# Moving a query projection beside V in a two-branch attention kernel: row layout, VectorE denominators, crossbar transposes, one output accumulation, and a new start

## The chip, the cores and the metric

The kernel runs on one core of one Trainium2 chip. The metric is device time in microseconds (us), the median over executions.

Names: PE is TensorE's matmuls, PEld its weight loads, DVE is VectorE, ACT is ScalarE, POOL is GpSimd, SP is SyncE, which here only issues DMAs. SPq is SP's instruction queue. PSUM is the memory that TensorE writes, in banks, which the kernel uses as tiles of up to 128 x 512 fp32 values; to evict a bank is to copy its result out with VectorE or ScalarE, after which it can be filled again. The granted clock is the share of full speed that TensorE was allowed, as the profile records it (PEclk). In the views, `pk`, `pq` and `kqt` are keys and queries, `KVT` the kv blocks, `oB` the banks of the windowed attention's results, `Ob` the evicted results and `OBT` their transposes, which a DMA makes; a name with `_ps` is a PSUM bank. `L153` is line 153 of that run's kernel.

## The reference

One input x (2048 x 1024) goes through two attention blocks, and a gate per row mixes the results.

```python
g = sigmoid((x * gate_w).sum(-1, keepdims=True))
a = A(x, A_wqkv, A_wo)      # linear attention, 32 heads of 32
b = B(x, B_wqkv, B_wo)      # 8 keys per query, dilation 2, softmax
return g * a + (1 - g) * b

# A: phi(t) = where(t > 0, t + 1, exp(t)) + 1e-6
#    kv = phi(k)^T v ;  z = sum over rows of phi(k)
#    o = phi(q) kv / (phi(q) . z + 1e-6) ; then @ wo
```

## The kernel before

TensorE's program is in manual order. It goes through these stages: A's keys (`pk`, from x transposed and half of `WkA` at a time), G = x^T pk, the blocks kv and the sums z, B's values V, B's keys and queries (`kq`) with the windowed attention woven in, A's queries, then the two output projections. All other engines' instructions are ordered by the framework's scheduler.

The start: the first tiles of x come through the DMA crossbar, which transposes them on the way; all of `WkA` is loaded at the same time from another queue.

```python
WkA = load_w("WkA", A_wqkv, D, eng=nc.scalar, parts=2)
for s0, s1_ in ((0, 128), (128, 256), (256, 512), (512, 1024), (1024, 1536), (1536, S)):
    nc.sync.dma_start_transpose(out=xT[:, :, s0:s1_], in_=rows(x, s0, s1_))
for t in range(0, NB, 4):
    nc.sync.dma_start(out=xrow[:, t:t + 4, :], in_=...)        # x again, as rows
```

The key stage. `phi` is one ScalarE and two VectorE instructions per PSUM bank. The z sums (`zacc`) and the gate's dot products (`gjunk`) come later in the program, but nothing keeps them there on VectorE:

```python
for half in range(2):
    for t in range(NB):
        pj = ps_1.tile([P, 512], F32, name="pk_ps", tag="p1")
        for kt in range(KT):
            nc.tensor.matmul(pj[:], lhsT=xT[...], rhs=WkA[half][:, kt, :], ...)
        phi(pk[:, t, half * 512:(half + 1) * 512], pj)
# ... G matmuls ...
for t in range(2, NB):
    nc.vector.tensor_tensor(out=zacc[:], in0=zacc[:], in1=pk[:, t, :], op=ALU.add)
for tb in range(NB):
    nc.vector.tensor_tensor_reduce(out=gjunk[:], in0=xrow[:, tb, :], in1=gw_row[:], ...)
```

The kv blocks, four in one PSUM bank:

```python
kvp = ps_1.tile([P, 4, P], F32, name="kv_ps", tag="p1")
for i in range(4):
    for kt in range(KT):
        nc.tensor.matmul(kvp[:, i, :], ...)
    nc.vector.tensor_tensor(out=KVT[:, half * 4 + i, :], in0=kvp[:, i, :], in1=bdmask[:], op=ALU.mult)
```

A's denominators take a matmul each, with the queries transposed (columns are rows of x); the two projections get a bank each:

```python
nc.tensor.matmul(den[:], lhsT=Zb[:, c, :], rhs=pq[b][:, c, :], start=True, stop=True)
nc.scalar.activation(out=ld[:], in_=den[:], func=ACT.Ln, bias=eps[:])
nc.scalar.activation(out=ld[:], in_=ld[:], func=ACT.Exp, scale=-1.0)
nc.vector.tensor_tensor(out=pqs[:, b, c, :], in0=pq[b][:, c, :], in1=ld[:], op=ALU.mult)
# ... output tile: side 0 = B, side 1 = A, one bank each
nc.scalar.activation(out=st["ob"][:], in_=st[0][:], func=ACT.Copy, scale=omgall[:, tb:tb + 1])
nc.vector.scalar_tensor_tensor(out=osb[:], in0=st[1][:], scalar=gall[:, tb:tb + 1], in1=st["ob"][:], ...)
```

The softmax here doesn't subtract the row's maximum and nothing guards it: scores larger than these inputs give would overflow.

## Time and profile before

| | before |
|---|---|
| median time | 518.13 us (518.01 to 519.95, 3 runs) |
| profiled span | 517.1 us |
| PE busy | 494.4 us, 96% |
| first stage (keys) ends | 72.75 us; its 256 matmuls at full rate would take 55.3 us |

The stretches of the kernel before, one line per stage. The columns are the stretch, its length, the busy time of each engine with its number of instructions, the granted TensorE clock, the DMA share and the rate. In order: keys, G, kv and z, V, k/q with attention, the last attention block with a quarter of A's queries, the rest of A's queries with the output, the tail.

```profile
core 0: us, PE busy (x) PEld busy (x) DVE busy (x) ACT busy (x) POOL busy (x), PEclk, DMA share, GB/s
0.00:72.75 72.75, 59.76 (x257) 25.78 (x258) 46.65 (x90) 19.20 (x31) 4.53 (x23) 0.98 0.89 249
72.75:128.00 55.25, 55.25 (x260) 25.11 (x258) 21.07 (x33) 9.97 (x18) 0.00 (x0) 1.00 0.06 20
128.00:136.50 8.50, 6.21 (x82) 5.48 (x79) 2.33 (x8) 0.58 (x1) 0.00 (x0) 1.00 0.42 135
136.50:195.30 58.80, 58.80 (x274) 26.64 (x273) 11.59 (x24) 18.37 (x32) 3.57 (x4) 1.00 0.32 94
195.30:333.30 138.00, 136.93 (x1509) 66.44 (x1508) 90.26 (x236) 73.71 (x103) 0.00 (x0) 1.00 0.25 59
333.30:354.40 21.10, 18.60 (x222) 8.94 (x220) 18.14 (x49) 12.33 (x18) 0.00 (x0) 1.00 0.16 30
354.40:513.30 158.90, 158.84 (x736) 71.81 (x734) 71.85 (x116) 75.24 (x120) 0.00 (x0) 1.00 0.08 27
513.30:517.10 3.80, 0.00 (x0) 0.00 (x0) 0.75 (x1) 0.00 (x0) 0.00 (x0) 1.00 0.10 35
```

The G stage gives the rate at full clock: 256 matmuls of 512 columns in 55.25 us, 0.216 us each. TensorE's waits, who waited for whom, with total (us), number of times and longest:

```profile
PE pk_ps L153 <- DMA xT<-in_A_x_dram: 12.0, 2, 9.6
PE kv_ps L191 <- DVE KVT L194: 2.3, 6, 0.4
PE oB L315 <- DVE Ob L324: 2.2, 2, 1.2
PE q_ps L362 <- DVE pq_3522 L140: 1.3, 2, 0.9
PE pk_ps L153 <- DVE pk L140: 0.8, 3, 0.4
```

The start on TensorE's timeline (start, length, what, then the idle time before it and what ended it). In between, the matmuls ran 427 ns apart, at half rate, until about 19.5 us.

```profile
9.55 3.41 PE L153 MATMUL pk_ps<-WkA_72,xT 128*128 128x512 bf16 x8 [9.55 <-DMA xT<-in_A_x_dram]
15.44 14.81 PE L153 MATMUL pk_ps<-WkA_72,xT 128*128 128x512 bf16 x60 [2.47 <-DMA xT<-in_A_x_dram]
```

This is a piece of the chain of waits, the work that ended last followed back (start, length, what):

```profile
27.77 5.42 DMA xrow<-in_A_x_dram
33.33 1.22 DVE gjunk L179
34.90 1.13 DVE gjunk L179
36.04 0.60 DVE pk L140
```

The chain does not run through TensorE here. It runs through the load of x as rows, then through VectorE, where a gate product (`gjunk`) stands ahead of key evictions (`pk`). TensorE itself hardly waited for VectorE (0.8 us in all), because it was late for other reasons.

### The profile page before, as it was taken

How to read it: one execution, taken by the hardware profiler on the slowest of the kernel's cores; microseconds unless marked ns; L12 is line 12 of the kernel's file. 1: busy time of each engine (PE TensorE's matmuls, PEld its weight loads, DVE VectorE, ACT ScalarE, POOL GpSimd, SP SyncE). 2: the span in 40 equal slices, each digit the busy share in tenths (PEclk: the TensorE clock that was granted, in tenths of full speed). 3: DMA queues.
4: the chain of work that ended last, by engine and by line, in shares of the span. 5: the costliest groups of instructions: out<-in, count | busy, mean ns of one | idle time of the engine just before them, and what ended most of it. 6: DMA issues, size and time to landing. Idle time of an engine off the chain costs nothing.

```text
span 517.1 us, 8148 instructions
## 1 busy us (share of the span) xinstructions
PE 494.4 (96%) x3328; PEld 230.2 (45%) x3328; DVE 262.6 (51%) x553; ACT 209.4 (40%) x323; POOL 8.1 (2%) x27
## 2 busy tenths in 40 slices
PE   2899999999899999999999999989999999999996
PEld 0344444444544444444544544444444444444443
DVE  0459999200331101577766777698742653454221
ACT  0223331111133332555564555566872364256111
POOL 3000000000200000000000000000000000000000
PEclk9899999999999999999999999999999999999999
DMA  8999820000432226011171111111010000001101
GB/s 196 239 345 354 269 82 1 0 0 1 163 91 75 92 78 206 10 34 29 33 189 33 31 28 34 35 28 23 1 41 32 10 31 32 22 10 42 41 32 41
DMA packets 61333, 39.21 MB, mean 76 GB/s; under 512 B 36400, under 2 KB 56880, under 8 KB 61296
## 3 DMA queue, kind: packets, MB, share of 16 engines
q1 hardware_dynamic: 59104, 36.34, 25.4%
q10 hardware_dynamic: 2112, 2.10, 1.5%
q8 instruction: 26, 0.43, 0.4%
q0 software_dynamic: 80, 0.26, 0.2%
q14 instruction: 11, 0.09, 0.1%
HBM read 21.23 MB, written 4.19 MB: 49 GB/s over the span
## 4 chain that ended last, share of the span: by engine, by line
PE 82%; DVE 9%; SPq 5%; DMA 3%; issue 1%; ACT 0%; DVEq 0%
PE d_ps L410 21%; PE kq_ps L266 21%; PE v_ps L237 11%; PE g_ps L165 11%; PE d_ps L362 8%; SPq L96 5%; PE oB L315 3%; DVE pk L140 2%; DVE gjunk L179 2%; DMA OBT<-Ob 2%; DVE e L139 1%; PE q_ps L362 1%; PE den L395 1%; DMA xrow<-in_A_x_dram 1%; PE pk_ps L153 1%; PE kv_ps L191 1%
## 5 line engine op out<-in xcount | busy, mean ns | idle before, releaser
L165 PE MATMUL g_ps<-pk,xrow 128*128 128x512 bf16 x256 | 55.4, 379 | 0.0
L420 DVE SCALAR_TENSOR_TENSOR osb<-d_ps,gall,ob 128x512 bf16<-128x512 f32 x32 | 24.0, 748 | 49.0 <-PE d_ps L410 42.6
L153 PEld LDWEIGHTS <-xT 128*128 128x128 bf16 x256 | 25.6, 101 | 46.7 <-DMA xT<-in_A_x_dram 12.7
L153 PE MATMUL pk_ps<-WkA_72,xT 128*128 128x512 bf16 x128 | 31.7, 409 | 12.8 <-DMA xT<-in_A_x_dram 12.0
L272 DVE CAST kqt<-kq_ps 128x512 bf16<-128x512 f32 x32 | 21.7, 679 | 42.5 <-PE kq_ps L266 42.2
L139 DVE TENSOR_SCALAR e<-e 128x512 f32<-128x512 f32 x64 | 26.6, 421 | 32.1 <-ACT e L138 32.1
L416 ACT ACTIVATE ob<-d_ps,omgall 128x512 f32<-128x512 f32 x32 | 21.9, 683 | 48.4 <-PE d_ps L410 48.4
L138 ACT ACTIVATE e<-pk_ps 128x512 f32<-128x512 f32 x32 | 19.1, 597 | 54.9 <-DVE pk L140 27.4
L410 PEld LDWEIGHTS <-OBT 128*128 128x128 bf16 x256 | 25.1, 98 | 30.2
L165 PEld LDWEIGHTS <-xrow 128*128 128x128 bf16 x256 | 25.0, 98 | 30.2
L410 PEld LDWEIGHTS <-pqs 128*128 128x128 bf16 x256 | 25.0, 98 | 30.2
L237 PEld LDWEIGHTS <-xT 128*128 128x128 bf16 x256 | 25.1, 98 | 30.0
L324 DVE TENSOR_TENSOR Ob<-oB,rd 128x256 bf16<-128x256 f32 x80 | 31.4, 393 | 3.8 <-DMA OBT<-Ob 2.6
L266 PE MATMUL kq_ps<-xT,WkB_103 128*128 128x512 bf16 x128 | 32.9, 380 | 0.0
L266 PE MATMUL kq_ps<-xT,WqB_570 128*128 128x512 bf16 x128 | 32.9, 379 | 0.0
L266 PE MATMUL kq_ps<-xT,WkB_101 128*128 128x512 bf16 x128 | 32.3, 379 | 0.0
L266 PE MATMUL kq_ps<-xT,WqB_568 128*128 128x512 bf16 x128 | 32.2, 379 | 0.0
L410 PE MATMUL d_ps<-WoA_93,pqs 128*128 128x512 bf16 x128 | 31.7, 379 | 0.0
L410 PE MATMUL d_ps<-WoB_3861,OBT 128*128 128x512 bf16 x128 | 31.2, 379 | 0.0
L410 PE MATMUL d_ps<-WoB_3859,OBT 128*128 128x512 bf16 x128 | 30.7, 379 | 0.0
L410 PE MATMUL d_ps<-WoA_95,pqs 128*128 128x512 bf16 x128 | 30.7, 379 | 0.0
L237 PE MATMUL v_ps<-WvB_99,xT 128*128 128x512 bf16 x128 | 30.6, 379 | 0.0
(161 smaller groups left out, 650.9 us busy)
## 6 DMA issues: line engine op xcount, KB each, us to landing
xrow<-in_A_x_dram SPq DMA_DIRECT2D x4, 1024.0 KB, 9.8
out_dram<-osb SPq DMA_DIRECT2D x32, 128.0 KB, 1.9
WkA_72<-in_A_wqkv_dram ACTq DMA_DIRECT2D x2, 512.0 KB, 6.2
WkA_75<-in_A_wqkv_dram ACTq DMA_DIRECT2D x2, 512.0 KB, 12.2
WvA_89<-in_A_wqkv_dram SPq DMA_DIRECT2D x1, 1024.0 KB, 15.4
WvA_91<-in_A_wqkv_dram SPq DMA_DIRECT2D x1, 1024.0 KB, 17.8
WoA_93<-in_A_wo_dram SPq DMA_DIRECT2D x1, 1024.0 KB, 12.4
WoA_95<-in_A_wo_dram SPq DMA_DIRECT2D x1, 1024.0 KB, 11.8
```

Source lines behind the costliest of these rows:

```text
L96: nc.sync.dma_start_transpose(out=xT[:, :, s0:s1_], in_=rows(x, s0, s1_))
L139: nc.vector.tensor_scalar(out=e[:], in0=e[:], scalar1=1.0, scalar2=1e-6, op0=ALU.min, op1=ALU.add)
L153: nc.tensor.matmul(pj[:], lhsT=xT[:, kt, t * P:(t + 1) * P], rhs=WkA[half][:, kt, :], start=(kt == 0), stop=(kt == KT - 1))
L165: nc.tensor.matmul(pj[:], lhsT=xrow[:, t, kt * P:(kt + 1) * P], rhs=pk[:, t, half * 512:(half + 1) * 512], start=(t == 0), stop=(t == NB - 1))
L237: nc.tensor.matmul(st["pj"][:], lhsT=xT[:, kt, t * P:(t + 1) * P], rhs=WvB[half][:, kt, :], start=(kt == 0), stop=(kt == KT - 1))
L266: nc.tensor.matmul(st["pj"][:], lhsT=W[c // 4][:, kt, (c % 4) * P:(c % 4 + 1) * P], rhs=xT[:, kt, cols], start=(kt == 0), stop=(kt == KT - 1))
L272: nc.vector.tensor_copy(out=kqt[:, 1, cols], in_=st["pj"][:])
L324: nc.vector.tensor_tensor(out=Ob[:, 2 * b:2 * b + m], in0=oBv[:, b, 0:m, :, 0:Dh], in1=rd[:, b, 0:m].broadcast_to([P, m, 4, Dh]), op=ALU.mult)
L362: nc.tensor.matmul(st["pj"][:], lhsT=WqA[c // 4][:, kt, (c % 4) * P:(c % 4 + 1) * P], rhs=xT[:, kt, cols], start=(kt == 0), stop=(kt == KT ...
L410: nc.tensor.matmul(st[side][:], lhsT=lhsT, rhs=W[half][:, c, :], start=(c == 0), stop=(c == KT - 1))
L416: nc.scalar.activation(out=st["ob"][:], in_=st[0][:], func=ACT.Copy, scale=omgall[:, tb:tb + 1])
L420: nc.vector.scalar_tensor_tensor(out=osb[:], in0=st[1][:], scalar=gall[:, tb:tb + 1], in1=st["ob"][:], op0=ALU.mult, op1=ALU.add)
```

## The change

Its intent is to bring TensorE to work earlier and to take work off it:

- **Start.** Two x tiles come as rows and are transposed on TensorE behind 20 warming matmuls. One half of `WkA` is loaded ahead of the remaining crossbar transposes, the other half after them. VectorE is put in program order from here to the end of the V and query stretch.
- **kv.** A bank per block; z by four 512-column matmuls.
- **Queries.** Twelve of A's 16 query tiles are computed beside V, in row layout, so that VectorE can form the denominators along the free dimension. They are spilled to DRAM and read back through the crossbar. Four tiles stay for the last attention block.
- **Output.** A's part is scaled by g/(1-g) beforehand, so both projections add up in one bank and one scaled eviction finishes a tile.

The core of the diff, cut:

```diff
+    load_rows(nc.scalar, 0, 1)
+    load_rows(nc.scalar, 1, 2)
+    WkA = load_w("WkA", A_wqkv, D, "wa", parts=4, only=(0,))
+    for t in range(2, NB):
+        nc.sync.dma_start_transpose(out=xT[:, :, t * P:(t + 1) * P], in_=rows(x, t * P, (t + 1) * P))
+    WkA += load_w("WkA", A_wqkv, D, "wa", only=(1,))
 ...
+            for i in range(5):
+                warm = ps_1.tile([P, 512], F32, name="warm", tag="p1")
+                for j in range(4):
+                    nc.tensor.matmul(warm[:, j * P:(j + 1) * P], lhsT=onesb[:], rhs=onesb[:], ...)
+            for t in range(2):
+                tp = ps_1.tile([P, KT, P], BF16, name="xt_ps", tag="p1")
+                for kt in range(KT):
+                    nc.tensor.transpose(out=tp[:, kt, :], in_=xrow[:, t, kt * P:(kt + 1) * P], identity=ident[:])
+                nc.vector.tensor_copy(out=xT[:, 0:4, ...], in_=tp[:, 0:4, :])
+                nc.scalar.copy(out=xT[:, 4:8, ...], in_=tp[:, 4:8, :])
+            s1.enter_context(tc.manual_schedule(engines={DVE}))
 ...
-                kvp = ps_1.tile([P, 4, P], F32, name="kv_ps", tag="p1")
+                kvp = ps_1.tile([P, P], F32, name="kv_ps", tag="p1")
 ...
+            def normalize(t, pq, pn, prod):
+                nc.vector.tensor_tensor(out=prod, in0=pq, in1=zrow[:], op=ALU.mult)
+                nc.vector.tensor_reduce(out=den[:], in_=prod..., axis=X, op=ALU.add)
+                nc.vector.tensor_scalar(out=den[:], in0=den[:], scalar1=1e-6, ...)
+                nc.vector.reciprocal(out=den[:], in_=den[:])
+                nc.vector.scalar_tensor_tensor(out=pn, in0=pq, scalar=ratio[:, t:t + 1], in1=den..., ...)
 ...
+            WoB = load_w("WoB", B_wo, 0, "wb")
+            nc.sync.dma_start_transpose(out=pqT[0][:], in_=pqd[0:512, :])
 ...
-                    nc.tensor.matmul(den[:], lhsT=Zb[:, c, :], rhs=pq[b][:, c, :], start=True, stop=True)
 ...
+                    nc.tensor.matmul(st["ps"][:, 0:n], lhsT=lhsT, rhs=W[...],
+                                     start=(side == 0 and c == 0), stop=(side == 1 and c == KT - 1))
+                    nc.scalar.activation(out=osb[:, 0:n], in_=st["ps"][:, 0:n], func=ACT.Copy,
+                                         scale=omg[:, tb:tb + 1])
```

## The prediction

> **What bounds it.** TensorE. The page's busy line gives PE 494.4 of 517.1 us, and warm 512-column matmuls start 0.216 us apart (256 of the G products take 55.25 us in the table of stretches). Lost, by TensorE's timeline and waits: first matmul at 9.55 us, 2.47 us before the second x tile; matmuls 427 ns apart until about 19.5 us, some 3.7 us (the Trainium skill, "TensorE: Matmul & The Clock Gate", Part 1, says half rate until about 3.4 us of sustained work; the 427 ns agree); 2.3 us waiting for KVT evictions; 2.2 us for oB; 1.3 us for q_ps; 3.8 us tail. The first stage ends at 72.75 us against 55.3 us of warm matmuls: 17.4 us lost.
>
> **What the change does.**
> 1. Start: two x tiles come as rows, are transposed on TensorE behind 20 warming matmuls; only half of WkA precedes the crossbar transposes. I expect the first key matmul at 6 to 7.5 us, clock loss 1 to 3 us, gaps up to 2 us. Crossbar tiles should follow every 1.05 to 1.35 us (512 rows took 4.2 us to issue before), faster than TensorE's 1.73 us per tile. First stage ends near 65: saves 7.5 us.
> 2. kv_ps gets a bank per block: the 2.3 us of KVT waits go. z becomes four 512-column matmuls, 0.9 for 1.7 us. Saves 3.2 in all.
> 3. 32 denominator matmuls go: 32 x 0.216 = 6.9 us off TensorE. ACT loses 64 activations (42 us), off the path.
> 4. 12 query tiles sit beside V. VectorE per 6.9 us of TensorE: phi 2 x 1.11, product 1.22, reduction about 1.2 (estimate: same 1024 elements as zacc, 1.216 us; the skill, "VectorE: DVE Perf Modes", the perf-mode tier table, has only 1x for tensor_reduce), small ones 0.45, scaling 1.22: about 6.3 us, 91%. With six banks TensorE should not wait. V+w2 58.7 us unchanged, queries 41.4 us.
> 5. Entering the k/q loop, VectorE still has some 5 us of normalising, while kq_ps has two banks, and WqB is loaded late into WvB's slots (landing took 5 to 6.5 us before): costs 0 to 3 us, say 1.2.
> 6. Last attention block: phi no longer competes on VectorE and its end overlaps output tiles: 21.1 us for 64 query matmuls plus attention becomes 17.6; transposes of pqd and WoB loads may delay OBT landings: net saving 3.
> 7. Output: one accumulation per tile, same 512 matmuls, half the evictions; ACT has 0.7 us per 3.45 us.  Smaller last store: saves 0.4; two 256-column halves cost about 0.5.
>
> Sum: 7.5 + 3.2 + 6.9 - 1.2 + 3 = 19.4 us; 518.1 becomes about 498.5, say 498 us (-3.9%), range 493 to 506. Chances: faster by over 2% 0.92, within 2% 0.07, slower 0.01.
>
> **What would show it.** Right: PE busy about 484 to 490 us; first key matmul before 8 us; first stage (first g_ps) starting at 62 to 69; no den matmuls; V+query stretch about 100 us with VectorE 85 to 95% busy in its query part and no PE wait there above 1 us; last attention plus late queries under 19 us.
> Wrong: waits of pk_ps on x or WkA in the first 35 us; PE waiting for VectorE in the V+query stretch; a gap over 3 us where kq_ps begins (on WqB or VectorE); oB waiting on Ob behind transposes; out_units waiting for pqT.
>
> **What would make it wrong.** The crossbar feeding tiles slower than 1.73 us each, WqB queued behind pqd stores (up to 10 us), a VectorE normalise over 6.9 us per tile, or OBT transposes stuck behind bulk loads in one queue.

## The result, and the profile after

The changed kernel took 496.08 us (median of 4 runs, 495.70 to 497.84), against 518.07 us for the kernel before. The ratio is 0.958, with a 95% interval of 0.954 to 0.961. Here and below a ratio is the mean time of one kernel's runs over the mean of the other's of the same rounds, so it is not quite the ratio of the medians.

The stretches of the changed kernel. The stages are the same up to kv and z; the fourth line is now V with twelve query tiles; then come k/q with attention, the last attention block with four query tiles, the output, and the tail.

```profile
core 0: us, PE busy (x) PEld busy (x) DVE busy (x) ACT busy (x) POOL busy (x), PEclk, DMA share, GB/s
0.00:62.80 62.80, 60.01 (x288) 29.00 (x294) 36.06 (x70) 20.96 (x34) 4.97 (x25) 1.00 1.02 280
62.80:118.00 55.20, 54.94 (x254) 25.05 (x257) 38.94 (x55) 9.59 (x17) 0.00 (x0) 1.00 0.06 20
118.00:122.49 4.49, 4.44 (x69) 3.96 (x68) 2.33 (x8) 0.98 (x2) 0.39 (x2) 1.00 0.34 106
122.49:222.64 100.15, 99.68 (x457) 45.39 (x464) 76.74 (x109) 37.89 (x65) 3.26 (x2) 1.00 0.31 102
222.64:359.40 136.76, 134.48 (x1483) 66.52 (x1508) 92.11 (x245) 73.72 (x103) 0.00 (x0) 1.00 0.19 46
359.40:379.60 20.20, 17.75 (x206) 8.43 (x208) 10.10 (x27) 11.69 (x19) 0.00 (x0) 1.00 0.57 131
379.60:490.40 110.80, 110.27 (x531) 51.76 (x538) 27.09 (x41) 26.73 (x41) 0.00 (x0) 1.00 0.26 68
490.40:493.90 3.50, 0.07 (x1) 0.00 (x0) 0.00 (x0) 0.47 (x1) 0.00 (x0) 0.84 0.07 20
```

Stage by stage, the two tables differ by this much:

| stage | before, us | after, us | saved, us |
|---|---|---|---|
| keys, with the start | 72.75 | 62.80 | 9.95 |
| G | 55.25 | 55.20 | 0.05 |
| kv and z | 8.50 | 4.49 | 4.01 |
| V, all queries but four tiles, denominators, output | 58.80 + 158.90 | 100.15 + 110.80 | 6.75 |
| k/q with attention | 138.00 | 136.76 | 1.24 |
| last attention block | 21.10 | 20.20 | 0.90 |
| tail | 3.80 | 3.50 | 0.30 |
| sum | 517.1 | 493.9 | 23.2 |

TensorE's waits after. The key matmuls' waits on x and the waits on KVT and on the queries' evictions are gone. The one on Ob is left, now in the last attention block (the timeline below has its time). Some matmul records are missing from this trace (3276 on its page, 3336 in the control run of the same kernel, which has PE busy 485.8 us), so short waits put down to "issue" are not read here.

```profile
PE oB_4252 L390 <- DVE Ob L396: 1.5, 1, 1.5
PE xt_ps L165 <- DMA xrow<-in_A_x_dram: 1.4, 2, 1.1
PE kq_ps L334 <- issue: 1.3, 8, 0.2
PE warm L161 <- DVE onesb L119: 1.1, 1, 1.1
PE oB_4202 L390 <- DVE Ob L396: 0.5, 1, 0.5
```

The start after, on TensorE's timeline: warming, two tiles transposed, and the first key matmul at 6.71 us, with no gap after it.

```profile
1.13 2.32 PE L161 MATMUL warm<-onesb 128*128 128x128 bf16 x20 [1.13 <-DVE onesb L119]
4.57 1.04 PE L165 MATMUL xt_ps<-ident,xrow 128*128 128x128 bf16 x8 [1.13 <-DMA xrow<-in_A_x_dram]
5.88 1.03 PE L165 MATMUL xt_ps<-ident,xrow 128*128 128x128 bf16 x8 [0.27 <-DMA xrow<-in_A_x_dram]
6.71 17.46 PE L175 MATMUL pk_ps<-WkA_77,xT 128*128 128x512 bf16 x75
```

The wait in the last attention block:

```profile
373.06 0.47 PE L390 MATMUL oB_4252<-V,PT_1879 128*128 128x33 bf16 x12 [1.51 <-DVE Ob L396]
```

### The profile page after: what moved, and what is told of

It reads as the page before. It is cut to its first block, busy times and chain, and to the rows that moved or that the text cites. A ratio compares the mean times of both kernels' runs of the same rounds, so it can differ in the third digit from the quotient of the medians.

```text
span 493.9 us, 8164 instructions
## 1 busy us (share of the span) xinstructions
PE 481.6 (98%) x3276; PEld 230.1 (47%) x3336; DVE 283.4 (57%) x550; ACT 182.0 (37%) x281; POOL 8.6 (2%) x29
## 4 chain that ended last, share of the span: by engine, by line
PE 96%; DMA 2%; issue 1%; DVE 0%; ACT 0%; SPq 0%; ACTq 0%; DVEq 0%
PE kq_ps L334 22%; PE d_ps L452 21%; PE pk_ps L175 11%; PE g_ps L198 11%; PE p_ps L257 11%; PE p_ps L291 8%; PE q_ps L291 1%; DMA OBT<-Ob 1%; DMA xrow<-in_A_x_dram 1%; PE kv_ps L216 1%; PE q_ps_4367 L452 1%; PE p_ps L246 1%; PE q_ps L452 1%; PE q_ps_4147 L291 0%; PE q_ps_4248 L291 0%
## 5 line engine op out<-in xcount | busy, mean ns | idle before, releaser
L457 ACT ACTIVATE osb<-d_ps,omg 128x512 bf16<-128x512 f32 (+1 forms) x31 | 20.9, 673 | 77.0 <-PE d_ps L452 72.5
L175 PEld LDWEIGHTS <-xT 128*128 128x128 bf16 x256 | 25.3, 99 | 30.4 <-issue 0.6
L257 PEld LDWEIGHTS <-xT 128*128 128x128 bf16 x256 | 25.0, 98 | 30.2
L291 PEld LDWEIGHTS <-xT 128*128 128x128 bf16 x256 | 24.2, 98 | 28.0
L373 DVE TENSOR_TENSOR PT_1878<-PT_1878,mask 128x672 bf16<-128x672 bf16 (+3 forms) x42 | 23.6, 571 | 17.0 <-ACT PT_1878 L371 16.7
L334 PE MATMUL kq_ps<-xT,WqB_1861 128*128 128x512 bf16 x120 | 31.8, 379 | 1.0 <-issue 0.6
L334 PE MATMUL kq_ps<-xT,WqB_1859 128*128 128x512 bf16 x124 | 31.7, 379 | 0.7 <-issue 0.5
L334 PE MATMUL kq_ps<-xT,WkB_1056 128*128 128x512 bf16 x122 | 31.6, 379 | 0.2
L334 PE MATMUL kq_ps<-xT,WkB_1054 128*128 128x512 bf16 x120 | 30.7, 379 | 0.4 <-issue 0.2
L373 DVE TENSOR_TENSOR PT_1879<-PT_1879,mask 128x672 bf16<-128x672 bf16 (+3 forms) x40 | 22.2, 564 | 15.3 <-ACT PT_1879 L371 15.1
L257 PE MATMUL p_ps<-WvB_112,xT 128*128 128x512 bf16 x126 | 30.6, 379 | 0.1
L257 PE MATMUL p_ps<-WvB_110,xT 128*128 128x512 bf16 x125 | 30.6, 379 | 0.1
L262 ACT CAST tmp<-p_ps 128x512 bf16<-128x512 f32 x32 | 18.8, 587 | 30.3 <-PE p_ps L257 27.9
L452 PEld LDWEIGHTS <-pqT_4425 128*128 128x128 bf16 x200 | 19.6, 98 | 22.1
L175 PE MATMUL pk_ps<-WkA_77,xT 128*128 128x512 bf16 x125 | 28.3, 386 | 0.2
L452 PE MATMUL d_ps<-WoB_4065,OBT 128*128 128x512 bf16 (+1 forms) x126 | 28.3, 366 | 0.1
```

What stands on the lines that cost most here:

```text
L175: nc.tensor.matmul(pj[:], lhsT=xT[:, kt, t * P:(t + 1) * P], rhs=WkA[half][:, kt, :], start=(kt == 0), stop=(kt == KT - 1))
L257: nc.tensor.matmul(st["pj"][:], lhsT=xT[:, kt, t * P:(t + 1) * P], rhs=WvB[half][:, kt, :], start=(kt == 0), stop=(kt == KT - 1))
L262: nc.scalar.copy(out=v[:, half * 16:(half + 1) * 16, 0:Dh], in_=st["pj"][:].rearrange("p (h e) -> p h e", h=16))
L291: nc.tensor.matmul(st["pj"][:], lhsT=xT[:, kt, t * P:(t + 1) * P], rhs=WqA[half][:, kt, :], start=(kt == 0), stop=(kt == KT - 1))
L334: nc.tensor.matmul(st["pj"][:], lhsT=W[c // 4][:, kt, (c % 4) * P:(c % 4 + 1) * P], rhs=xT[:, kt, cols], start=(kt == 0), stop=(kt == KT - 1))
L373: nc.vector.tensor_tensor(out=ptv[:, hs], in0=ptv[:, hs], in1=m[:, None, :].broadcast_to([P, 2, W_]), op=ALU.mult)
```

## The experiments

Twelve kernels ran. Names beginning with b_ are edits of the kernel before, names beginning with a_ are edits of the changed kernel. The kernel before had medians of 517.93 us on one chip, where all b_ runs but b_startorder were timed, and of 518.31 and 518.46 us on another, where the rest were; the last two medians share eleven of their runs. On that second chip the last four kernels were timed some minutes after the control, not beside it. Most single parts are worth less than 2%, so the table gives the intervals.

| run | edit | median, us | ratio to before (95%) | first g_ps, us |
|---|---|---|---|---|
| b_start | start alone | 520.56 | 1.003 (1.000 to 1.007) | 75.1 |
| b_startorder | start and VectorE order | 509.02 | 0.982 (0.979 to 0.984) | 63.1 |
| b_kvbank | a bank per kv block | 515.01 | 0.993 (0.990 to 0.996) | 73.5 |
| b_noden | 31 denominator matmuls out | 511.85 | 0.987 (0.984 to 0.990) | 73.3 |
| b_nochain | work behind them out | 519.91 | 1.003 (0.999 to 1.007) | 72.8 |
| a_again | none (control) | 496.16 | 0.957 (0.955 to 0.960) | 62.7 |
| a_nowarm | no warming | 495.63 | 0.956 (0.954 to 0.958) | 63.1 |
| a_xbar01 | tiles 0, 1 by crossbar | 502.78 | 0.969 (0.967 to 0.972) | 67.6 |
| a_wkafull | all of WkA first | 497.65 | 0.960 (0.957 to 0.963) | 64.9 |
| a_queues | bulk moved from the OBT queue | 496.17 | 0.958 (0.955 to 0.960) | 62.9 |
| a_twoacc | two accumulations again | 497.54 | 0.960 (0.958 to 0.963) | 64.0 |
| a_red2 | reduction done twice | 503.79 | 0.973 (0.970 to 0.976) | 63.0 |

### Parts of the change, alone, in the kernel before

**b_start.** The loads, warming and transposes of the change were put into the kernel before; VectorE was left to the scheduler.

> The kernel before with the change's start alone (first two x tiles as rows, transposed on TensorE behind 20 warming matmuls; half of WkA ahead of the crossbar transposes). Theory: the start is worth what the two traces differ by in their first stage, 72.75 - 62.8 = 9.95 us, independent of the rest: first g_ps at 62.5 to 64 us, time 9 to 10.5 us under before. Rival: part of those 10 us comes from the VectorE order that the change also sets (gate and z work moved out of this stage; PE waited 0.8 us for VectorE there): then first g_ps comes 1 us or more later than in the changed kernel, gain under 9 us.

It gained nothing: 520.56 us, 0.3% slower. TensorE's two longest waits in it:

```profile
PE pk_ps L175 <- DVE pk L151: 8.5, 1, 8.5
PE kv_ps L213 <- DVE KVT L216: 2.3, 6, 0.4
```

VectorE's timeline around the wait:

```profile
21.14 0.69 DVE L151 SCALAR_TENSOR_TENSOR pk<-pk_ps,e 128x512 bf16<-128x512 f32 x1
35.53 1.22 DVE L201 CUSTOM_DVE_ANT_0 gjunk<-xrow,gw_row 128x1024 bf16<-128x1024 bf16 x1 [13.70 <-DMA xrow<-in_A_x_dram]
```

TensorE started at 7.4 us and had filled its banks by about 30 us. VectorE had stopped evicting keys at 21.8 us: next in its queue was a gate product, whose x rows landed only at 35.5 us. The evictions behind it were ready but could not pass. The Trainium skill ("TensorE: Matmul & The Clock Gate", the table at its head) gives VectorE's queue as strictly first in, first out, and this trace agrees: 13.70 us idle with evictions waiting. After this idle time the matmuls ran slow for a while: the granted clock was 0.55 between 35 and 40 us and 0.76 between 40 and 45. The rival was right, and by far more than the 1 us it named.

**b_startorder.** One line more: VectorE in program order in the first part.

```diff
+            s1.enter_context(tc.manual_schedule(engines={DVE}))
             pk = big.tile([P, NB, D], BF16, name="pk", tag="pkO")
```

> The kernel before with the change's start, as in b_start, and in addition the program's own order on VectorE in the first part (the gate sums and z sums come after all key evictions, not between them). b_start alone gained nothing: TensorE waited 8.5 us for key evictions that stood in VectorE's queue behind a gate sum, which waited for x rows until 35.5 us. Theory: start and VectorE order together make the gain, neither alone: no wait of pk_ps for VectorE over 0.5 us, first g_ps at 62.5 to 64 us, 9 to 10.5 us under before. Rival: something else in the older kernel (x rows, weights) then stops the first stage: gain under 5 us.

It took 509.02 us, 9.4 us under before by the medians. The wait was gone and G began at 63.08 us:

```profile
54.66 8.58 PE L177 MATMUL pk_ps<-WkA,xT 128*128 128x512 bf16 x39
63.08 12.25 PE L189 MATMUL g_ps<-pk,xrow 128*128 128x512 bf16 x56
```

So the start and the VectorE order are one change in effect. The start without the order is worth nothing. The order without the start was not run; from the trace of before it can hardly be worth more than the 0.8 us that TensorE waited for key evictions there, but that is argued, not shown.

**b_kvbank.**

```diff
-                kvp = ps_1.tile([P, 4, P], F32, name="kv_ps", tag="p1")
                 for i in range(4):
+                    kvp = ps_1.tile([P, P], F32, name="kv_ps", tag="p1")
 ...      # matmuls and product on kvp[:] instead of kvp[:, i, :]
```

> The kernel before with one PSUM bank per kv block instead of four blocks in one bank; z as before. Theory: the six 0.38 us gaps at kv_ps go, 2.3 us faster, the kv and z stretch 8.5 us becomes about 6.2. Rival: the gaps turn into a wait elsewhere (KVT products at the first w2 matmul): under 1 us.

It took 515.01 us, 2.9 us under before by the medians (3.6 us by the ratio, of which 2.3 us were expected), and the KVT wait is not in its list any more. The Trainium skill ("PSUM — Partial Sum Buffer", PSUM bank collisions raise a hardware error) says that two engines must not touch the same bank and 32-partition quadrant at once, so a program has to order them. The six waits of 0.38 us in the trace before fit that, and they go with the shared bank. The edit also splits one tile into four, so the runs do not tell an ordering by bank from one by tile.

The gain beyond 2.3 us may have to do with the clock, but what makes the clock dip is not settled. Of the 11 runs of the kernel before in that session, the three with a granted clock of 0.989 to 0.993 took 520.9 to 521.4 us, the eight above that 516.7 to 519.2 us. Without these three the mean of before is 2.6 us above b_kvbank's, near the 2.3 us expected. No run of b_kvbank was below 0.995, and none of the changed kernel below 0.999. One trace caught such a dip: in b_nochain the clock was 0.52 just after the kv and z stage (136 to 140 us).

**b_noden and b_nochain.** The first takes out 31 of 32 denominator matmuls and keeps what follows them; the second keeps the matmuls and takes out what follows. Both give wrong denominators. The comparison with the reference lets denominators that belong to other rows and heads pass.

```diff
 b_noden
-                    nc.tensor.matmul(den[:], lhsT=Zb[:, c, :], rhs=pq[b][:, c, :], start=True, stop=True)
+                    if not one:      # first call only
+                        nc.tensor.matmul(one[0][:], ...)
 b_nochain
-                    nc.scalar.activation(out=ld[:], in_=den[:], func=ACT.Ln, bias=eps[:])
-                    nc.scalar.activation(out=ld[:], in_=ld[:], func=ACT.Exp, scale=-1.0)
-                    nc.vector.tensor_tensor(out=pqs[:, b, c, :], in0=pq[b][:, c, :], in1=ld[:], op=ALU.mult)
+                    nc.vector.tensor_copy(out=pqs[:, b, c, :], in_=pq[b][:, c, :])
```

> The kernel before with 31 of the 32 denominator matmuls taken out; every Ln reads the one that is left, so the result is wrong on purpose; ScalarE and VectorE work unchanged. Theory: TensorE time alone counts: 31 x 0.216 = 6.7 us faster. Rival: the ScalarE/VectorE chain behind the denominators paces these stages: under 2 us.

> The kernel before with the denominator matmuls kept, but the 64 ScalarE activations behind them (42 us busy) removed and the VectorE multiply replaced by a plain copy: wrong result on purpose. Theory: off the critical path, within 1 us of before, ScalarE busy some 42 us less, VectorE some 10 us less. Rival: that work limits: 3 us or more faster.

b_noden took 511.85 us: 6.1 us less by the medians, 6.8 by the ratio, against 31 x 0.216 = 6.7 us of matmul time (5.8 us if the three runs of before at a low clock are left out). b_nochain took 519.91 us, not faster. The first line of its page, for ScalarE 209.4 us before:

```profile
PE 498.8 (96%) x3328; PEld 231.6 (45%) x3328; DVE 250.5 (48%) x553; ACT 170.5 (33%) x259; POOL 8.1 (2%) x27
```

ScalarE lost 38.9 us of work and VectorE 12.1 us, and the time did not fall. Only the matmuls counted.

### Parts of the start, undone in the changed kernel

**a_again, a_nowarm, a_xbar01, a_wkafull** ran together.

> The changed kernel unaltered, as control for the runs beside it: 495.5 to 498 us, spread under 1 us.

The control took 496.16 us (494.92 to 497.32), a spread of 2.4 us where under 1 us was expected.

```diff
 a_nowarm
-            for i in range(5):
-                warm = ...                    # 20 matmuls
```

> The changed kernel without its 20 warming matmuls. In the changed kernel only about three key matmuls ran 427 ns apart. Theory: the 2.3 us of warming count toward the busy time that releases the clock, so some 10 of the first key matmuls run at half rate and it costs 1 to 2.5 us, all before the second tile ends. Rival: the transposes and the first products warm the array about as soon: under 0.5 us.

Without warming it took 495.63 us, 0.5 us less than the control, which is inside the spread: the rival was right. TensorE could not have begun before 4.5 us anyway, since the x rows had not landed. After the warming ended at 3.45 us it stood idle until 4.57 us in the changed kernel's trace. In the profiled pair G began 0.4 us later without warming (63.06 against 62.67 us), so a gain of that size is not excluded. In the traces of kernels that have the warming, the number of first key matmuls at half rate still varied: about 3 in a_again, 8 in a_twoacc and 10 in a_wkafull (counted by weight loads 0.43 us apart; the granted clock reads 1.00 there, so it does not show them), whose first key matmuls started within 0.25 us of each other; without warming it was about 6. The Trainium skill ("TensorE: Matmul & The Clock Gate", Part 1) says that the window that decides is free-running and that the number of matmuls at half rate varies from run to run; these counts agree.

```diff
 a_xbar01
-    load_rows(nc.scalar, 0, 1)
-    load_rows(nc.scalar, 1, 2)
+    for t in range(2):
+        nc.sync.dma_start_transpose(out=xT[:, :, t * P:(t + 1) * P], in_=rows(x, t * P, (t + 1) * P))
     WkA = load_w("WkA", A_wqkv, D, "wa", parts=4, only=(0,))
 ...
-    load_rows(nc.sync, 2, 4)
+    load_rows(nc.sync, 0, 4)
 ...
-            for t in range(2):
-                tp = ps_1.tile([P, KT, P], BF16, name="xt_ps", tag="p1")   # TensorE transposes
```

> The changed kernel with tiles 0 and 1 of x transposed by the crossbar, first in the queue, ahead of the half of WkA; warming kept. Theory: transposing on TensorE is what brings the first product forward: first key matmul at 8.5 us or later with the array cold again, 3 to 5 us slower. Rival: what counted is that 2 MB of WkA no longer share the engines with the first transposes: first key matmul at 6.5 to 8 us, under 2 us slower.

It took 502.78 us, 6.6 us slower than the control, yet the first key matmul came at 7.12 us, where the rival had it. Neither theory had the reason:

```profile
7.12 1.01 PE L168 MATMUL pk_ps<-WkA,xT 128*128 128x512 bf16 x2 [3.69 <-DMA WkA<-in_A_wqkv_dram]
8.39 1.01 PE L168 MATMUL pk_ps<-WkA,xT 128*128 128x512 bf16 x2 [0.25 <-DMA WkA<-in_A_wqkv_dram]
11.50 12.67 PE L168 MATMUL pk_ps<-WkA,xT 128*128 128x512 bf16 x50 [2.11 <-DMA WkA<-in_A_wqkv_dram]
```

x was there by 5.2 us, but the four parts of `WkA`, now behind two transposes in one queue, were not. G began 4.9 us later than in the control. Another 2.5 us of the profiled run, the slowest of its six, were lost in the last attention block (3.0 us of waits on Ob and a clock of 0.93 there), which the edit does not touch. So the run shows that this order of loads is worse. It does not show what TensorE's transposes alone are worth, because the edit moved `WkA` too (and loads two more tiles as rows later).

```diff
 a_wkafull
     WkA = load_w("WkA", A_wqkv, D, "wa", parts=4, only=(0,))
+    WkA += load_w("WkA", A_wqkv, D, "wa", only=(1,))
     for t in range(2, NB):
         nc.sync.dma_start_transpose(...)
-    WkA += load_w("WkA", A_wqkv, D, "wa", only=(1,))
```

> The changed kernel with both halves of WkA ahead of the 14 crossbar transposes instead of one. Theory: the transposes of tiles 2 on start about 1 MB later (some 4 us at 250 GB/s), tile 2 was needed at about 10.2 us and had little slack, so TensorE waits 2 to 4 us for x after tile 1: first g_ps at 65 to 67. Rival: transposes and loads overlap on 16 engines and the slack is enough: under 1 us.

It took 497.65 us, 1.5 us more than the control, and G began 2.2 us later, which looks like the theory. But the matmuls' list of waits has none for x tiles. The weight loads, which fetch the x tile here, waited for x twice, 1.0 us in all; in the control not once:

```profile
PEld L175 <- DMA xT<-in_A_x_dram: 1.0, 2, 0.6
```

The larger part is the clock: about 10 matmuls at half rate instead of 3, 7 x 0.21 = 1.5 us, and the first key matmul came 0.23 us later. So x, 1 MB later, was just about late, by half a microsecond (what is left of the 2.2 us), not by 2 to 4. Whether the later clock release is chance or follows from the edit is open.

### The output, the queue and VectorE's margin

**a_queues.** The only sizeable wait left on TensorE was in the last attention block. There one OBT transpose took 5.5 us to land (median 2.3), behind a 1 MB transpose of spilled queries and a 1 MB load of half of `WoB`.

```diff
-            WoB = load_w("WoB", B_wo, 0, "wb")
+            WoB = load_w("WoB", B_wo, 0, "wb", eng=nc.scalar)
-            nc.sync.dma_start_transpose(out=pqT[0][:], in_=pqd[0:512, :])
+            nc.sync.dma_start_transpose(out=pqT[0][:], in_=pqd[0:P, :])   # the rest after the block
```

> The changed kernel with WoB loaded from ScalarE's queue instead of SyncE's, and only the first of the twelve spilled query tiles transposed during the last attention block, the other eleven after it. In the changed kernel an OBT transpose took 5.5 us to land there behind a 1 MB transpose and a 1 MB load in the same queue, VectorE waited for the buffer and TensorE 1.5 us for VectorE. Theory: the OBT transposes land in 2 to 3 us again and TensorE's oB waits go: 1.5 to 2.5 us faster than the changed kernel. Rival: the engines are shared whatever the queue, the wait stays or TensorE waits for the second query tile: within 0.5 us.

It took 496.17 us, the same as the control. Its TensorE waits after the start:

```profile
PE oB L390 <- DVE PT L373: 0.8, 2, 0.5
PE q_ps L291 <- DVE Ob L396: 0.7, 1, 0.7
```

Two things happened. In the last block the waits fell from 2.0 to 0.7 us, and from its first query matmul to the first output matmul it took 18.7 us instead of 20.2. But two OBT transposes still took 5.8 and 5.1 us to land while that load ran from the other queue. The Trainium skill ("DMA: Bandwidth & Descriptors", Queues, rings and completion order) says that every DMA engine takes turns between the queues; the trace agrees in so far as another queue did not keep the load out of the way. And the gain was given back by the same cause at another place. The load of the first half of `WoB`, now at the head of ScalarE's queue, started in the k/q loop at 287.2 us, 2.6 us earlier than in the control; three OBT transposes around it took 3.7 to 6.4 us to land; VectorE waited 2.0 us for one of them before an Ob product, with the mask products that TensorE needed behind it; and TensorE waited 0.8 us. The loop took 137.9 us instead of 136.8. The experiment gives no faster kernel.

**a_twoacc.**

```diff
-                    if side == 0 and c == 0:
-                        st["ps"] = bank()
+                    if c == 0:
+                        st[side] = bank()
 ...
+                    nc.scalar.activation(out=ob[:, 0:n], in_=st[0][:, 0:n], func=ACT.Copy, scale=omg[...])
+                    nc.vector.scalar_tensor_tensor(out=osb[:, 0:n], in0=st[1][:, 0:n], scalar=omg[...], in1=ob[...], ...)
```

> The changed kernel with the two outputs accumulated in two banks again and joined by ScalarE and VectorE (31 more evictions of 0.7 us and the joins of 0.75 us, as in the kernel before). Theory: one accumulation only spares idle engines: within 1 us of the changed kernel, about 0.5 us slower at the end of the last tile. Rival: the extra evictions and banks hold TensorE: 3 us or more slower.

It took 497.54 us, 1.4 us more than the control. In the profiled pair 1.3 us of the difference lie in the first stage, where nothing was edited (about 8 matmuls at half rate instead of 3). The last attention block was 0.75 us shorter, with 1.1 us of waits on Ob instead of 1.9. The first output tile was 1.06 us longer, and there the edit shows: TensorE waited 0.9 us for VectorE's join of the two banks, a wait that the control does not have. The rest of the output took the same time. So in this pair the single accumulation spared about 1 us, once, and nothing per tile; the medians can't tell it from the 2.4 us spread.

**a_red2.** The reduction in `normalize` was issued twice.

```diff
                 nc.vector.tensor_reduce(out=den[:], in_=prod..., axis=X, op=ALU.add)
+                nc.vector.tensor_reduce(out=den[:], in_=prod..., axis=X, op=ALU.add)
```

> The changed kernel with each denominator's VectorE reduction done twice, 1.22 us more per query tile: VectorE needs about 7.7 us where TensorE needs 6.9 (it needs 6.5 now by the trace). Theory: VectorE now lags by some 0.8 us per tile over 12 tiles; six banks take part of it, the rest shows as TensorE waits near the end of the V and query stretch or at kq_ps: 3 to 10 us slower. Rival: banks and later slack take it all: under 1 us.

It took 503.79 us, 7.6 us more than the control. The wait came where k/q begins:

```profile
224.67 1.90 PE L336 MATMUL kq_ps<-xT,WqB 128*128 128x512 bf16 x8
227.13 1.89 PE L336 MATMUL kq_ps<-xT,WkB 128*128 128x512 bf16 x8 [0.56 <-ACT kqt L340]
233.65 3.34 PE L336 MATMUL kq_ps<-xT,WqB 128*128 128x512 bf16 x8 [4.63 <-DVE kqt L342]
```

During the 83 us of V and queries TensorE did not wait once: the six banks there hid VectorE's growing lag. It showed when the banks went down to two and VectorE owed their evictions behind its backlog: 0.6 + 4.6 us of waits, and then eight matmuls in 3.34 us, at half rate, 1.5 us lost. In the changed kernel VectorE needs 6.5 us per query tile where TensorE needs 6.9. There, VectorE's timeline at the same place shows the scheduler slipping a k/q eviction between two steps of the last denominators:

```profile
225.75 1.22 DVE L278 TENSOR_REDUCE den<-tmp 128x32 f32<-128x1024 f32 x1
226.88 0.68 DVE L340 CAST kqt<-kq_ps 128x512 bf16<-128x512 f32 x1
227.48 0.17 DVE L280 TENSOR_SCALAR den<-den 128x32 f32<-128x32 f32 x1
```

## Why the prediction was right, point by point

The predicted 498 us, with a range of 493 to 506, met 496.08 us. The predicted saving was 19.4 us; the measured one is 22.0 us by the medians. The three edits tried alone in the kernel before (b_startorder 9.4, b_noden 6.1, b_kvbank 2.9 us by the medians) add up to 18.4 of the 22.0 us. Some terms were off, and one held for an incomplete reason. That the sum came so close is in part luck: the start, kv and the entry to k/q came out better than predicted by 2.5, 0.8 and 1.2 us, k/q brought 1.2 us that was not predicted, and the last attention block came out 2.1 us worse.

1. **Start: 7.5 us predicted, 9.95 measured; size roughly right, reason incomplete.** The first key matmul came at 6.71 us (6 to 7.5 predicted), there was no gap (up to 2 us predicted), and the loss to the clock was under 1 us (1 to 3 predicted). But the step named only loads, transposes and warming. b_start has all of these and gains nothing. The gain needs VectorE in program order, which the step did not mention although the diff has it and the chain of waits before ran through the gate products. Warming, which the step counted, is worth nothing that can be measured. The crossbar was also closer to its limit than said: the median tile took 1.32 us to issue (1.05 to 1.35 predicted), but some took up to 3.34 us, and all 14 took 23.1 us, 1.65 us each on average, against TensorE's 1.73.
2. **kv and z: 3.2 us predicted, 4.0 measured.** Right; b_kvbank shows the larger part alone.
3. **Denominator matmuls: 6.9 us predicted, 6.75 measured.** b_noden and b_nochain show that it is the matmuls, not the chain behind them.
4. **VectorE beside V: 6.3 us per tile predicted, 6.5 measured, and no TensorE wait.** Right. VectorE was 86% busy in the query part (71.33 of 83.34 us; 85 to 95% predicted). The reduction took 1.22 us for 1024 elements; the prediction took about 1.2 us from the single 1x rate in the Trainium skill ("VectorE: DVE Perf Modes", the perf-mode tier table) and from the zacc sum over as many elements in the trace before. a_red2 shows how near the edge it is: 1.22 us more per tile cost 7.6 us.
5. **Entry to k/q: a cost of 1.2 us predicted, none seen.** `WqB`'s first half was issued at 217.5 us, landed in 5.3 us and was needed at 224.2 us; the k/q eviction was put between the denominators' steps. The saving of 1.24 us in the loop is not from the change as far as the runs show: in b_startorder and b_noden, with the older attention code, it takes 136.8 us too, in b_kvbank 138.0, while the profiled run of before held one late OBT transpose of 8.4 us, behind two 1 MB loads of `WoB`.
6. **Last attention block: a saving of 3 us predicted, 0.9 measured.** This is the term that was most off. The step expected 17.6 us for the block (under 19 as the sign of being right) and it took 20.2. It named the risk (OBT landings behind bulk transfers) but priced it too low: 2.0 us of waits on Ob remained, which the prediction had listed as a sign of being wrong. In a_queues, with 0.7 us of waits, the block took 18.7 us, so the waits are the larger part of the miss.
7. **Output and tail: a net cost of 0.1 us predicted; the tail came out 0.3 us shorter.** Smaller than the runs can tell apart; the profiled pair of a_twoacc puts the single accumulation at about 1 us.

## What to carry to other kernels

When a stage is late, follow the chain of waits before pricing its parts: an engine that is only slightly waited for can have a queue order that becomes the limit the moment the other delay is removed, so an earlier start must come with an eviction order that lets it through. Price removed work by whether it sits on the limiting engine: 31 matmuls of 6.7 us gave 6.1 us by the medians, while 51 us of work on two other engines gave nothing. In a_red2 a backlog on the evicting engine stayed hidden while there were six banks and was paid at the next stage, which had two: look there first.

## What the Trainium skill lacked or had wrong

- "TensorE: Matmul & The Clock Gate", Part 1: it has the release of the clock and its variation, both seen here (about 3, 8 and 10 matmuls at half rate with nearly the same start). It lacks what a warming burst is worth when a pause follows it: 2.3 us of warming and 1.1 us of idle saved nothing measurable (495.63 us without, 496.16 us with).
- "DMA: Bandwidth & Descriptors", Latency and other measured facts: it gives 261 GB/s for a transposing DMA with a non-contiguous middle dimension. Issued by SyncE in pieces of 512 rows, 1 MB took 4.2 us here (median, kernel before), 250 GB/s, which is near. In pieces of 128 rows, 256 KB took 1.32 us (median, changed kernel), 198 GB/s, and 1.65 us on average, 159 GB/s. The row gives no dependence on the size of the piece.
- "VectorE: DVE Perf Modes", the perf-mode tier table: it has no row for scalar_tensor_tensor, which took 0.69 us for 512 elements and 1.28 us for 1024 here, no faster per element than the tensor_reduce that it does list (1.22 us for 1024).
